# Attention transposes as 64x64 products with the identity, decoding parts one step later, six squares on GpSimd

## The chip, the cores and the metric

The kernel runs on one core of a Trainium2 chip. PE (TensorE) multiplies into PSUM, eight banks of 512 f32 columns on 128 partitions; ACT (ScalarE), DVE (VectorE) and POOL (GpSimd) work on SBUF, the first two on PSUM too; SP (SyncE) issues the transfers. The metric is the device time of one execution in microseconds, the median over runs. "us" is microseconds, "0.90 us" a duration, and a bare position such as 254.95 is microseconds from the start of the span.

## The reference

q, k and v are float32; the four weight arrays are float64, and the kernel reads them as pairs of 32-bit words, which it decodes. Three stages follow each other:

```python
# q, k, v: 8 batches, 8 heads, 576 positions, 64 features; blocks of 64 positions
scores = q_c @ k_c.T / sqrt(64)                 # per batch, head and block
attn = exp(scores - max); attn /= sum(attn) + 1e-9
x = (attn @ v_c)                                # as 4608 tokens x 512 features
# first dense pair: 512 -> 2048 -> 512
x = (max(x @ w_in1, 0) ** 2) @ w_out1
# second dense pair, with another activation
h = x @ w_in2
out = where(h >= 1, h, where(h <= -1, 0, (h + 1) ** 2 / 4)) @ w_out2
```

## The kernel before

**Tokens and slots.** A tile is 128 tokens (two blocks of 64) with all eight heads; there are 36. A unit is a tile's half of four heads (`UT` = 2 units a tile). The first dense product (`plain_h`) works on blocks of 512 tokens, `NBL` = 9 of them, by 16 slices of 128 hidden features; one (block, slice) takes two slots of six matmuls each. The loop at the end walks over slots: in each it issues first what `pe_slot` has put there (matmuls of the dense layers), then what `at_slot` has put there, in the order in which it was put, then one `decode()` where the slot is in `CALLS`. The engines take their instructions in this order. Nothing reorders it.

**Head.** Tiles 0 to 3 (`T0_` = 4) are worked before slot 0, unit by unit, in `head(i)` for i = 0 to 7 and `head_end()`. In step i PE takes `att_a` of unit i+1 (transposes of q and k), `att_b` of i (scores), `att_c` of i-1 (transposes of the attention weights) and `att_d` of i-2 (weights times v); ACT takes `att_ae` (copies of the transposed q and k into qkT), `att_exp`, `att_ce` (copy of the transposed weights into atT) and `att_xh` (result into the high part xh); DVE takes the maxima, the reciprocal of the sums and `att_xl` (low part xl = result - xh); POOL normalizes (`att_n`; the last unit's on DVE). `PARTS[i]` and `LOADS[i]` follow at the end of step i.

**Decoding.** `w_in1` comes as float64 words in 16 pieces. Each piece is turned into a high and a low part in five steps: `piece_u` (ACT: abs; DVE: two operations), `piece_l` (DVE; from part 3 on it also issues the load of a later piece), `piece_b` (DVE), `piece_h` (ACT: rounding copy), `piece_c` (DVE: difference). Pieces 0 to 3 are decoded in the head by `PARTS`, the others by `decode()`.

**Overlapped stage.** From slot 0 on tiles 4 to 35 are worked between the plain matmuls, a tile every `PER` = 8 slots. With g = 6 + 8(t - 5) for tile t: `tile_a` at g-8, `tile_ae` at g-5, `tile_b` at g, `tile_exp` at g and g+1, `tile_n` at g+4, `tile_c` and `tile_ce` at g+6, `tile_d` and `tile_x` at g+8. In slot g PE therefore takes `tile_d` of t-1, `tile_b` of t and `tile_a` of t+1 in a row, in slot g+6 `tile_c` of t alone. Tile 4 has times of its own: scores in slot 1, `tile_c` in slot 10, `tile_d` in slot 12, where tile 5's `tile_c` follows. From slot 28 on the other weights are decoded too, and stored as sums in DRAM.

**PSUM.** Two banks take tag `t`: two buffers of one bank, which psA (transposed q or k) and psC (transposed weights) share. Two banks take `qk` (psB, the scores; in the head the last unit's psD also), two take `d` (psD, the result), two the plain products ph.

**Squares.** `plain_h` ends with relu on ACT and a square, on ACT while the slot is below `U0` = 28 (14 slices), then on POOL; SP stores the result.

Behind slot 288 the rest of the dense layers follows; the change does not touch it.

Of the kernel before, what the change touches and what calls it, by code (L numbers as in the profile page):

```python
# [34 lines left out]
def chunk_attention_moe_moe2(ctx, tc, q, k, v, w_in1, w_out1, w_in2, w_out2, out):  # L35
# [246 lines left out]
    def of_tile(name, u, shape, bufs=1):  # L282

        if (name, u // UT) not in ttile:
            ttile[name, u // UT] = ep.tile(shape, F32, tag=name, name=name, bufs=bufs)
        return ttile[name, u // UT]

    def qkT_of(u):
        t = u // UT
        if t % 2 and t < T0_ and ("qkT", t) not in ttile:  # L290
            ttile["qkT", t] = mp.tile([P, UT, 2, NP, P], F32, tag="q4", name="qkT", padded_shape=[P, 2, 2, 2, P])
        return of_tile("qkT", u, [P, UT, 2, NP, P])
# [39 lines left out]
    def load_v(t):  # L332
        for r, n, b, s in runs_of(t):
            nc.sync.dma_start(out=vt[t % NV][r:r + n], in_=v[b, :, s:s + n, :].rearrange("h s d -> s h d"))

    def att_a(u):

        qkn, h0 = qks[u // UT], u % UT * HU
        pt = pa.tile([P, 2, NP, P], F32, tag="t", name="psA", bufs=2)
        for i in range(2):  # L340
            for p in range(NP):
                nc.tensor.transpose(
                    pt[:, i, p, :], qkn[i][:, h0 + 2 * p:h0 + 2 * p + 2, :].rearrange("p h d -> p (h d)"), ident
                )
        att[u] = pt

    def att_ae(u):
        qkT = qkT_of(u)[:, u % UT]
        pt = att.pop(u)
        nc.scalar.activation(out=qkT[:, 0], in_=pt[:, 0], func=AF.Copy, scale=SCALE)  # L350
        nc.scalar.copy(qkT[:, 1], pt[:, 1])

    def tile_a(t, halves=(0, 1)):

        for i in halves:
            att[t, "a", i] = pt = pa.tile([P, UT, NP, P], F32, tag="t", name="psA", bufs=2)
            for h in range(0, H, 2):
                nc.tensor.transpose(  # L358
                    pt[:, h // HU, h // 2 % NP, :], qks[t][i][:, h:h + 2, :].rearrange("p h d -> p (h d)"), ident
                )  # L360

    def tile_ae(t, halves=(0, 1)):
        qkT = qkT_of(t * UT)
        for i in halves:
            pt = att.pop((t, "a", i))
            if i == 0:
                nc.scalar.activation(out=qkT[:, :, 0], in_=pt, func=AF.Copy, scale=SCALE)
            else:
                nc.scalar.copy(qkT[:, :, 1], pt)

    def att_b(u):

        pt = pa.tile([P, 2, 512], F32, tag="qk", name="psB")
        scores(pt[:, :, 0:2 * CH], qkT_of(u)[:, u % UT])
        att[u] = maxima(pt, 2)

    def scores(pt, qkT):
        for p in range(NP):
            for e in range(2):
                for c in range(2):  # L380
                    nc.tensor.matmul(  # L381
                        pt[rows(p), e, c * CH:(c + 1) * CH],
                        qkT[rows(e), 0, p, rows(c)],
                        qkT[rows(e), 1, p, rows(c)],
                        start=True,
                        stop=True,
                    )
# [30 lines left out]
    def tile_b(t):  # L418
        pt = pa.tile([P, 2, 512], F32, tag="qk", name="psB")
        for i in range(UT):  # L420
            scores(pt[:, :, i * 2 * CH:(i + 1) * 2 * CH], qkT_of(t * UT)[:, i])
        att[t, "b"] = maxima(pt, UT * 2)

    def tile_exp(t, e):
# [6 lines left out]
    def att_n(u):  # L431
        normalize(*att[u], nc.gpsimd if u < T0_ * UT - 1 else nc.vector)

    def turned(pt, s, n):
        for e in range(2):
            nc.tensor.transpose(  # L436
                pt[:, e].rearrange("k p t -> k (p t)"), s[:, e, 2 * n:2 * n + 2].rearrange("q c k -> q (c k)"), ident
            )

    def att_c(u):  # L440
        pt = pa.tile([P, 2, NP, CH], F32, tag="t", name="psC", padded_shape=[P, HU, 2, CH], bufs=2)
        turned(pt, s_of(u), u % UT)
        att[u] = pt

    def att_ce(u):
        nc.scalar.copy(at_of(u)[:, u % UT], att.pop(u))

    def tile_c(t):
        att[t, "c"] = pt = pa.tile([P, UT, 2, NP, CH], F32, tag="t", name="psC", bufs=2)
        for i in range(UT):  # L450
            turned(pt[:, i], s_of(t * UT), i)

    def tile_ce(t):
        nc.scalar.copy(at_of(t * UT), att.pop((t, "c")))

    def att_d(u):

        pt = pa.tile([P, 2, 512], F32, tag="qk" if u == T0_ * UT - 1 else "d", name="psD")
        weigh(pt, u)
        att[u] = pt  # L460
# [13 lines left out]

    def att_xh(u):
        att[u] = x_ops(att[u], u)
        att[u][0]()

    def att_xl(u):
        att.pop(u)[1]()  # L480
# [8 lines left out]
        )  # L489

    def tile_d(t):
        att[t, "d"] = pt = pa.tile([P, 2, 512], F32, tag="d", name="psD")
        for i in range(UT):
            weigh(pt, t * UT + i, i * NP * CH)

    def tile_x(t):
        pt = att.pop((t, "d"))
        ops = [x_ops(pt, t * UT + i, i * NP * CH) for i in range(UT)]
        for n in range(2):
            for o in ops:  # L500
                o[n]()
# [19 lines left out]
    def plain_h(j, fi, part):  # L521
        n = blocks[j][1]
        if part == 0:
            hs[j, fi] = pa.tile([P, n], F32, tag=f"h{(j * NF + fi) % 2}", name="ph")
        ph = hs[j, fi]
        xh, xl = xs[j, part]
        for i in range(2):
            kt = 2 * part + i
            for a, (wi, x) in enumerate(((0, xh), (1, xh), (0, xl))):
                nc.tensor.matmul(  # L530
                    ph,
                    win[fi][wi][:, kt * P:(kt + 1) * P],
                    x[:, i, :],
                    start=(kt == 0 and a == 0),
                    stop=(kt == KT - 1 and a == 2),
                )
        if part == 0:
            return
        del hs[j, fi]
        g = rt(RG[n_r[0] % len(RG)], [P, n], "g")  # L540
        n_r[0] += 1
        nc.scalar.activation(out=g, in_=ph, func=AF.Relu)  # L542
        if cur[0] < U0:
            nc.scalar.square(g, g)
        else:
            nc.gpsimd.tensor_tensor(out=g, in0=g, in1=g, op=ALU.mult)  # L546
        kh, kk = divmod(fi, HF)
        b0 = blocks[j][0]
# [244 lines left out]
    with tc.manual_schedule():  # L793
# [27 lines left out]
        def tiles_until(j):  # L821
# [269 lines left out]
```

## Time and profile before

| | us |
|---|---|
| median of 3 runs (lowest to highest) | 1563.29 (1563.06 to 1563.56) |
| profiled execution | 1563.68 |
| span of the profiled execution | 1561.9 |
| PE busy, share of the span | 1543.7, 99% |
| DVE busy | 1082.7, 69% |
| ACT busy | 871.0, 56% |
| POOL busy | 315.2, 20% |

The span runs from the first to the last instruction; the profiled execution has 1.8 us around it. A PE row's duration includes the emptying of the array, so rows overlap; what a matmul costs in a row of them is the distance between two starts. Names are those of the program's tiles; L579 is a line of the kernel.

### The profile page before, as it was taken

What the parts mean: (1) busy time and instruction counts of PE and PEld (TensorE: products, weight loads), DVE (VectorE), ACT (ScalarE), POOL (GpSimd) and SP (SyncE); (2) the same over time, 40 slices, a digit from 0 to 9 for tenths busy, and PEclk for the clock granted to TensorE, in tenths of its full rate; (3) what the DMA queues carried; (4) which work ended last, traced back from release to release, by engine and by line L of the source; (5) the groups of instructions that cost most, each with busy time, mean ns of one, the idle gap of its engine ahead of it and who ended that gap; (6) DMA issues with size and microseconds to landing.
All of it is one profiled execution on the core that took longest, in us unless ns stands there. A gap on an engine that the chain in (4) does not pass through costs nothing.

```text
span 1561.9 us, 26712 instructions
## 1 busy us (share of the span) xinstructions
PE 1543.7 (99%) x9504; PEld 1360.0 (87%) x9504; DVE 1082.7 (69%) x1405; ACT 871.0 (56%) x1768; POOL 315.2 (20%) x351
## 2 busy tenths in 40 slices
PE   7999999999999999999999999999999999999998
PEld 5788888888888889999999889999999889999998
DVE  5866766676452576777677657767675787878876
ACT  6876666666552444444444566767676534444442
POOL 1036666664334100000000122322210000000000
PEclk9999999999999999999999999999999999999999
DMA  9889999999998972716376775665679982744633
GB/s 209 239 244 301 303 301 308 303 311 299 264 286 242 357 213 85 224 49 199 106 225 198 235 269 175 213 231 192 214 263 296 326 230 69 177 120 117 179 70 48
DMA packets 440677, 339.43 MB, mean 217 GB/s; under 512 B 209632, under 2 KB 410336, under 8 KB 440544
## 3 DMA queue, kind: packets, MB, share of 16 engines
q1 hardware_dynamic: 436832, 337.27, 71.3%
q8 instruction: 75, 1.23, 0.3%
q10 hardware_dynamic: 3712, 0.46, 0.2%
q14 instruction: 58, 0.48, 0.1%
HBM read 195.04 MB, written 142.61 MB: 216 GB/s over the span
## 4 chain that ended last, share of the span: by engine, by line
PE 95%; ACT 2%; DVE 1%; DMA 1%; issue 0%; SPq 0%; POOL 0%; POOLq 0%; ACTq 0%
PE X L579 38%; PE ph L530 24%; PE V L579 19%; PE W L579 9%; PE psA L358 2%; PE psD L467 1%; PE psB L381 1%; PE psC L436 1%; DMA ws<-in_moe_w_in_dram 1%; ACT s L399 1%; DMA w<-w 0%; ACT ih L129 0%; ACT ih L179 0%; ACT g L542 0%; DVE wy L133 0%
## 5 line engine op out<-in xcount | busy, mean ns | idle before, releaser
L579 PE MATMUL X<-oh,w 128*128 128x448 f32 (+1 forms) x1920 | 548.5, 367 | 0.0
L566 ACT CAST oh<-gr 128x896 fp32r<-128x896 f32 (+1 forms) x280 | 270.0, 965 | 319.4 <-PE X L579 142.0
L569 DVE TENSOR_TENSOR ol<-gr,oh 128x896 fp32r<-128x896 f32 (+1 forms) x280 | 312.7, 1118 | 176.3 <-ACT oh L566 163.4
L579 PEld LDWEIGHTS X<-oh,w 128*128 128x128 f32 x1920 | 359.8, 187 | 36.4
L579 PE MATMUL X<-ol,w 128*128 128x448 f32 (+1 forms) x960 | 353.6, 368 | 0.4 <-DVE ol L569 0.4
L579 PE MATMUL V<-oh,w 128*128 128x448 f32 (+1 forms) x960 | 274.2, 367 | 0.0
L530 PE MATMUL ph<-xh,ih 128*128 128x512 f32 x576 | 232.1, 403 | 0.0
L530 PE MATMUL ph<-xl,ih 128*128 128x512 f32 x576 | 225.8, 392 | 0.0
L530 PE MATMUL ph<-xh,il 128*128 128x512 f32 x576 | 225.5, 391 | 0.0
L546 POOL TENSOR_TENSOR g<-g 128x512 f32<-128x512 f32 x130 | 164.6, 1267 | 230.5 <-ACT g L542 205.3
L579 PEld LDWEIGHTS V<-oh,w 128*128 128x128 f32 x960 | 179.9, 187 | 18.2
L579 PEld LDWEIGHTS X<-ol,w 128*128 128x128 f32 x960 | 180.2, 188 | 15.8 <-DVE ol L569 0.8
L573 DVE TENSOR_TENSOR gr<-gr,gr 128x896 f32<-128x896 f32 (+1 forms) x160 | 177.7, 1110 | 1.6 <-DMA gr<-g 1.6
L579 PE MATMUL V<-ol,w 128*128 128x448 f32 (+1 forms) x480 | 176.7, 368 | 0.0
L213 POOL TENSOR_TENSOR lc<-lc 128x128 f32<-128x128 f32 x64 | 37.3, 594 | 495.9 <-DVE t L659 364.6
L579 PE MATMUL W<-oh,w 128*128 128x448 f32 (+1 forms) x480 | 137.1, 367 | 0.0
L542 ACT ACTIVATE g<-ph 128x512 f32<-128x512 f32 x144 | 86.1, 598 | 85.4 <-PE ph L530 57.3
L530 PEld LDWEIGHTS ph<-xl,ih 128*128 128x128 f32 x576 | 108.7, 189 | 23.7
L530 PEld LDWEIGHTS ph<-xh,ih 128*128 128x128 f32 x576 | 108.9, 189 | 21.2 <-ACT g L542 0.2
L530 PEld LDWEIGHTS ph<-xh,il 128*128 128x128 f32 x576 | 109.2, 190 | 20.7
L653 ACT ACTIVATE t<-c,half 128x448 f32<-128x448 f32 (+1 forms) x120 | 81.0, 680 | 49.9 <-DVE c L639 48.7
L399 ACT ACTIVATE s<-psB,m 128x64 f32<-128x64 f32 x288 | 86.4, 318 | 25.3 <-DVE m L393 25.2
(75 smaller groups left out, 1748.1 us busy)
## 6 DMA issues: line engine op xcount, KB each, us to landing
gr<-g SPq DMA_DIRECT2D x128, 448.0 KB, 4.8
w<-w SPq DMA_DIRECT2D x168, 256.0 KB, 5.2
g<-t SPq DMA_DIRECT2D x128, 224.0 KB, 3.0
wu<-in_moe_w_out_dram SPq DMA_DIRECT2D x64, 256.0 KB, 4.9
gr<-g SPq DMA_DIRECT2D x32, 512.0 KB, 6.7
w<-wh SPq DMA_DIRECT2D x32, 448.0 KB, 4.5
w<-wl SPq DMA_DIRECT2D x32, 448.0 KB, 5.1
ws<-in_moe_w_in_dram SPq DMA_DIRECT2D x16, 512.0 KB, 5.3
```

Source lines behind the costliest of these rows:

```text
L213: nc.gpsimd.tensor_tensor(out=c[:, o], in0=c[:, x], in1=c[:, z], op=op)
L358: nc.tensor.transpose(pt[:, h // HU, h // 2 % NP, :], qks[t][i][:, h:h + 2, :].rearrange("p h d -> p (h d)"), ident)
L381: nc.tensor.matmul(pt[rows(p), e, c * CH:(c + 1) * CH], qkT[rows(e), 0, p, rows(c)], qkT[rows(e), 1, p, rows(c)], start=True, stop=True,)
L399: nc.scalar.activation(out=s[:, e, c], in_=sc[:, e, c], func=AF.Exp, bias=m[:, e, c:c + 1], accum_out=z[:, e, c:c + 1],)
L530: nc.tensor.matmul(ph, win[fi][wi][:, kt * P:(kt + 1) * P], x[:, i, :], start=(kt == 0 and a == 0), stop=(kt == KT - 1 and a == 2),)
L542: nc.scalar.activation(out=g, in_=ph, func=AF.Relu)
L546: nc.gpsimd.tensor_tensor(out=g, in0=g, in1=g, op=ALU.mult)
L566: nc.scalar.copy(t[0], raw)
L569: nc.vector.tensor_tensor(out=t[1], in0=raw, in1=f(t[0]), op=ALU.subtract)
L573: eng.tensor_tensor(out=o, in0=x, in1=z, op=ALU.subtract)
L579: nc.tensor.matmul(o, wt_[:, wi, c, :], x[:, i, :], start=first and a == 0, stop=last and a == 2, skip_group_check=True,)
L653: nc.scalar.activation(out=t, in_=h, func=AF.Square, bias=half, scale=0.5)
```

## The change

All transposes of the attention, which PE did with its transpose of a 128x128 block, become products: each 64x64 quarter of the data is the stationary operand, and 64 columns of the identity are moved through, in the quarter of the array that belongs to the data's partitions (r) and to the result's (e). The result of row half r goes to bank r. psA becomes one tile of two banks that all tiles use (q in columns 0 to 255, k in 256 to 511); psC is gone, its products go to columns 256 to 511 of the one psD, whose columns 0 to 255 take the result. The layout of qkT changes to match, and the scores' loop has its column block outermost. The `PARTS` list begins with an empty step, so that each part comes one head step later, and `piece_b` of piece 3 goes into `head_end`. Squares below slot `SQ0` = 12 (six slices) go to POOL.

```diff
     def qkT_of(u):
...
-            ttile["qkT", t] = mp.tile([P, UT, 2, NP, P], F32, tag="q4", name="qkT", padded_shape=[P, 2, 2, 2, P])
+            ttile["qkT", t] = mp.tile([P, 2, UT, NP, P], F32, tag="q4", name="qkT", padded_shape=[P, 2, 2, 2, P])
+    def turn(pt, src, o):
+        for r in range(2):
+            for e in range(2):
+                nc.tensor.matmul(
+                    pt[rows(e), r, o:o + CH], src(r, e), ident[rows(r), rows(r)], start=True, stop=True
+                )
     def att_a(u):
         qkn, h0 = qks[u // UT], u % UT * HU
-        pt = pa.tile([P, 2, NP, P], F32, tag="t", name="psA", bufs=2)
         for i in range(2):
             for p in range(NP):
-                nc.tensor.transpose(
-                    pt[:, i, p, :], qkn[i][:, h0 + 2 * p:h0 + 2 * p + 2, :].rearrange("p h d -> p (h d)"), ident
-                )
+                turn(psA, lambda r, e: qkn[i][rows(r), h0 + 2 * p + e, :], u % UT * 256 + (i * NP + p) * CH)
     def att_ae(u):
...
+        qkT = qkT_of(u)
+        for i in range(2):
+            o = u % UT * 256 + i * NP * CH
+            src = psA[:, :, o:o + NP * CH].rearrange("d r (p t) -> d r p t", p=NP)
+            copy_qk(i, qkT[:, i, u % UT].rearrange("d p (r t) -> d r p t", r=2), src)
     def tile_a(t, halves=(0, 1)):
         for i in halves:
-            att[t, "a", i] = pt = pa.tile([P, UT, NP, P], F32, tag="t", name="psA", bufs=2)
             for h in range(0, H, 2):
-                nc.tensor.transpose(
-                    pt[:, h // HU, h // 2 % NP, :], qks[t][i][:, h:h + 2, :].rearrange("p h d -> p (h d)"), ident
-                )
+                turn(psA, lambda r, e: qks[t][i][rows(r), h + e, :], i * 256 + h // 2 * CH)
     def scores(pt, qkT):
-        for p in range(NP):
-            for e in range(2):
-                for c in range(2):
+        for c in range(2):
+            for p in range(NP):
+                for e in range(2):
                     nc.tensor.matmul(
...
-    def turned(pt, s, n):
+    def turned(u):
+        s, n = s_of(u), u % UT
         for e in range(2):
-            nc.tensor.transpose(
-                pt[:, e].rearrange("k p t -> k (p t)"), s[:, e, 2 * n:2 * n + 2].rearrange("q c k -> q (c k)"), ident
-            )
+            turn(psD, lambda r, c: s[rows(r), e, 2 * n + c, :], 256 + (2 * n + e) * CH)
+    def copied(at, o, n):
+        nc.scalar.copy(
+            at.rearrange("k e p t -> k p e t"), psD[:, :, o:o + n * CH].rearrange("k p (e t) -> k p e t", t=CH)
+        )
     def tile_c(t):
-        att[t, "c"] = pt = pa.tile([P, UT, 2, NP, CH], F32, tag="t", name="psC", bufs=2)
         for i in range(UT):
-            turned(pt[:, i], s_of(t * UT), i)
+            turned(t * UT + i)
     def att_d(u):
-        pt = pa.tile([P, 2, 512], F32, tag="qk" if u == T0_ * UT - 1 else "d", name="psD")
-        weigh(pt, u)
-        att[u] = pt
+        weigh(psD, u, u % UT * NP * CH)
     def tile_d(t):
-        att[t, "d"] = pt = pa.tile([P, 2, 512], F32, tag="d", name="psD")
         for i in range(UT):
-            weigh(pt, t * UT + i, i * NP * CH)
+            att_d(t * UT + i)
...
-        if cur[0] < U0:
+        if SQ0 <= cur[0] < U0:
             nc.scalar.square(g, g)
         else:
             nc.gpsimd.tensor_tensor(out=g, in0=g, in1=g, op=ALU.mult)
...
-    U0, UPER = 28, 5
+    U0, UPER, SQ0 = 28, 5, 12
...
+        psA = pa.tile([P, 2, 512], F32, tag="t", name="psA")
+        psD = pa.tile([P, 2, 512], F32, tag="d", name="psD")
...
         PARTS = (
+            (),
             ((piece_u, 0), (piece_l, 0)),
...
             ((piece_l, 3), (piece_c, 2)),
-            ((piece_b, 3),),
         )
...
             att_xl(u - 2)
+            piece_b(3)
             att_c(u)
             att_d(u - 1)
```

## Rows read from the trace of the kernel before

**Rows 1.** The page's first part: busy us (share of the span) and instructions.
```profile
PE 1543.7 (99%) x9504; PEld 1360.0 (87%) x9504; DVE 1082.7 (69%) x1405; ACT 871.0 (56%) x1768; POOL 315.2 (20%) x351
```

**Rows 2.** Busy time by stretch: from:to, length, engines, granted clock, DMA share, GB/s.
```profile
20.00:30.00 10.00, 8.81 (x114) 5.91 (x113) 8.13 (x21) 9.09 (x44) 1.84 (x3) 1.00 0.96 215
50.00:60.00 10.00, 7.78 (x37) 6.28 (x36) 8.49 (x17) 9.23 (x29) 0.00 (x0) 0.93 0.98 248
200.00:300.00 100.00, 100.00 (x930) 82.64 (x933) 67.79 (x102) 66.40 (x202) 65.74 (x78) 1.00 0.98 302
```

**Rows 3.** PE's waits in 0 to 100 us: total us, times, longest.
```profile
PE psC L436 <- ACT qkT L367: 2.2, 1, 2.2
```

**Rows 4.** PE timeline, one period: start, us, line, operation, tiles, shapes, count.
```profile
254.95 0.39 PE L530 MATMUL ph<-xl,ih 128*128 128x512 f32 x1
255.18 0.60 PE L436 MATMUL psC<-ident,s 128*128 128x128 f32 x4
...
255.85 0.40 PE L530 MATMUL ph<-xh,il 128*128 128x512 f32 x1
...
258.16 0.39 PE L530 MATMUL ph<-xl,ih 128*128 128x512 f32 x1
258.48 0.69 PE L467 MATMUL psD<-atT,vt 64*64 64x64 f32 x32
258.99 0.75 PE L381 MATMUL psB<-qkT 64*64 64x64 f32 x32
259.67 1.09 PE L358 MATMUL psA<-ident,qkn 128*128 128x128 f32 x8
...
260.84 0.40 PE L530 MATMUL ph<-xh,il 128*128 128x512 f32 x1
...
268.78 0.60 PE L436 MATMUL psC<-ident,s 128*128 128x128 f32 x4
```

**Rows 5.** PE timeline around the last psD.
```profile
475.24 0.39 PE L530 MATMUL ph<-xl,ih 128*128 128x512 f32 x1
475.56 0.69 PE L467 MATMUL psD<-atT,vt 64*64 64x64 f32 x32
476.18 0.50 PE L530 MATMUL ph<-xh,ih 128*128 128x512 f32 x1
476.52 0.39 PE L530 MATMUL ph<-xh,il 128*128 128x512 f32 x1
```

**Rows 6.** PE timeline cut at 258.62: the first two rounds of psD.
```profile
258.48 0.34 PE L467 MATMUL psD<-atT,vt 64*64 64x64 f32 x8
```

**Rows 7.** PE timeline at slot 10.
```profile
55.71 0.39 PE L530 MATMUL ph<-xl,ih 128*128 128x512 f32 x1
58.31 0.91 PE L436 MATMUL psC<-ident,s 128*128 128x128 f32 x4 [2.22 <-ACT qkT L367]
...
62.01 0.40 PE L530 MATMUL ph<-xh,il 128*128 128x512 f32 x1
```

**Rows 8.** Groups by line and shape: busy us, mean ns, idle before and its releasers.
```profile
L546 POOL TENSOR_TENSOR g<-g 128x512 f32<-128x512 f32 x130 | 164.6, 1267 | 230.5 <-ACT g L542 205.3 <-DMA g<-g 9.0 <-DMA w<-w 6.7
...
L544 ACT ACTIVATE g<-g 128x512 f32<-128x512 f32 x14 | 8.9, 633 | 0.4
```

**Rows 9.** Timeline of all engines at slot 12.
```profile
63.89 0.66 PE L436 MATMUL psC<-ident,s 128*128 128x128 f32 x4
...
64.74 0.76 DVE L488 TENSOR_TENSOR xl<-psD,xh 128x256 fp32r<-128x256 f32 x2 [2.58 <-ACT xh L487]
```

**Rows 10.** Timeline of all engines in the first unit.
```profile
3.79 0.29 PEld L342 LDWEIGHTS psA<-ident,qkn 128*128 128x128 f32 x2 [0.28 <-DMA qkn<-in_k_dram]
...
4.52 0.38 ACT L350 ACTIVATE qkT<-psA 128x256 f32<-128x256 f32 x1 [2.51 <-PE psA L342]
```

**Rows 11.** PE timeline at the end of the head.
```profile
33.93 0.66 PE L436 MATMUL psC<-ident,s 128*128 128x128 f32 x2
...
35.72 0.80 PE L530 MATMUL ph<-xh,ih 128*128 128x512 f32 x1
```

More of the change, by code (lines that the diff above doesn't have):

```diff
@@ L290, in qkT_of @@
         if t % 2 and t < T0_ and ("qkT", t) not in ttile:
-            ttile["qkT", t] = mp.tile([P, UT, 2, NP, P], F32, tag="q4", name="qkT", padded_shape=[P, 2, 2, 2, P])
-        return of_tile("qkT", u, [P, UT, 2, NP, P])
+            ttile["qkT", t] = mp.tile([P, 2, UT, NP, P], F32, tag="q4", name="qkT", padded_shape=[P, 2, 2, 2, P])
+        return of_tile("qkT", u, [P, 2, UT, NP, P])
     def s_of(u):
@@ L334, in load_v, with copy_qk @@
             nc.sync.dma_start(out=vt[t % NV][r:r + n], in_=v[b, :, s:s + n, :].rearrange("h s d -> s h d"))
+    def turn(pt, src, o):
[4 more added lines that the diff above has]
+                )
     def att_a(u):
         qkn, h0 = qks[u // UT], u % UT * HU
-        pt = pa.tile([P, 2, NP, P], F32, tag="t", name="psA", bufs=2)
         for i in range(2):
             for p in range(NP):
-                nc.tensor.transpose(
-                    pt[:, i, p, :], qkn[i][:, h0 + 2 * p:h0 + 2 * p + 2, :].rearrange("p h d -> p (h d)"), ident
-                )
-        att[u] = pt
+                turn(psA, lambda r, e: qkn[i][rows(r), h0 + 2 * p + e, :], u % UT * 256 + (i * NP + p) * CH)
     def att_ae(u):
[L348 to L351, printed above, removed]
+        qkT = qkT_of(u)
[3 more added lines that the diff above has]
+            copy_qk(i, qkT[:, i, u % UT].rearrange("d p (r t) -> d r p t", r=2), src)
+    def copy_qk(i, out, src):
+        if i == 0:
+            nc.scalar.activation(out=out, in_=src, func=AF.Copy, scale=SCALE)
+        else:
+            nc.scalar.copy(out, src)
     def tile_a(t, halves=(0, 1)):
         for i in halves:
-            att[t, "a", i] = pt = pa.tile([P, UT, NP, P], F32, tag="t", name="psA", bufs=2)
             for h in range(0, H, 2):
-                nc.tensor.transpose(
-                    pt[:, h // HU, h // 2 % NP, :], qks[t][i][:, h:h + 2, :].rearrange("p h d -> p (h d)"), ident
-                )
+                turn(psA, lambda r, e: qks[t][i][rows(r), h + e, :], i * 256 + h // 2 * CH)
     def tile_ae(t, halves=(0, 1)):
@@ L364, in tile_ae @@
         for i in halves:
[L365 to L369, printed above, removed]
+            src = psA[:, :, i * 256:(i + 1) * 256].rearrange("d r (p t) -> d r p t", t=CH)
+            copy_qk(i, qkT[:, i].rearrange("d u p (r t) -> d r (u p) t", r=2), src)
     def att_b(u):
         pt = pa.tile([P, 2, 512], F32, tag="qk", name="psB")
-        scores(pt[:, :, 0:2 * CH], qkT_of(u)[:, u % UT])
+        scores(pt[:, :, 0:2 * CH], qkT_of(u)[:, :, u % UT])
         att[u] = maxima(pt, 2)
     def scores(pt, qkT):
-        for p in range(NP):
-            for e in range(2):
-                for c in range(2):
+        for c in range(2):
+            for p in range(NP):
+                for e in range(2):
                     nc.tensor.matmul(
@@ L420, in tile_b @@
         for i in range(UT):
-            scores(pt[:, :, i * 2 * CH:(i + 1) * 2 * CH], qkT_of(t * UT)[:, i])
+            scores(pt[:, :, i * 2 * CH:(i + 1) * 2 * CH], qkT_of(t * UT)[:, :, i])
         att[t, "b"] = maxima(pt, UT * 2)
@@ L432, in att_n @@
         normalize(*att[u], nc.gpsimd if u < T0_ * UT - 1 else nc.vector)
-    def turned(pt, s, n):
+    def turned(u):
+        s, n = s_of(u), u % UT
         for e in range(2):
-            nc.tensor.transpose(
-                pt[:, e].rearrange("k p t -> k (p t)"), s[:, e, 2 * n:2 * n + 2].rearrange("q c k -> q (c k)"), ident
-            )
+            turn(psD, lambda r, c: s[rows(r), e, 2 * n + c, :], 256 + (2 * n + e) * CH)
[3 more added lines that the diff above has]
+        )
     def att_c(u):
-        pt = pa.tile([P, 2, NP, CH], F32, tag="t", name="psC", padded_shape=[P, HU, 2, CH], bufs=2)
-        turned(pt, s_of(u), u % UT)
-        att[u] = pt
+        turned(u)
     def att_ce(u):
-        nc.scalar.copy(at_of(u)[:, u % UT], att.pop(u))
+        copied(at_of(u)[:, u % UT], 256 + u % UT * 2 * CH, 2)
     def tile_c(t):
-        att[t, "c"] = pt = pa.tile([P, UT, 2, NP, CH], F32, tag="t", name="psC", bufs=2)
         for i in range(UT):
-            turned(pt[:, i], s_of(t * UT), i)
+            turned(t * UT + i)
     def tile_ce(t):
-        nc.scalar.copy(at_of(t * UT), att.pop((t, "c")))
+        copied(at_of(t * UT).rearrange("k u e p t -> k (u e) p t"), 256, UT * 2)
     def att_d(u):
-        pt = pa.tile([P, 2, 512], F32, tag="qk" if u == T0_ * UT - 1 else "d", name="psD")
-        weigh(pt, u)
-        att[u] = pt
+        weigh(psD, u, u % UT * NP * CH)
     def weigh(pt, u, o=0):
@@ L475, in att_xh @@
     def att_xh(u):
-        att[u] = x_ops(att[u], u)
+        att[u] = x_ops(psD, u, u % UT * NP * CH)
         att[u][0]()
@@ L491, in tile_d @@
     def tile_d(t):
-        att[t, "d"] = pt = pa.tile([P, 2, 512], F32, tag="d", name="psD")
         for i in range(UT):
-            weigh(pt, t * UT + i, i * NP * CH)
+            att_d(t * UT + i)
     def tile_x(t):
-        pt = att.pop((t, "d"))
-        ops = [x_ops(pt, t * UT + i, i * NP * CH) for i in range(UT)]
+        ops = [x_ops(psD, t * UT + i, i * NP * CH) for i in range(UT)]
         for n in range(2):
```

## The prediction

> **What bounds the kernel now.** I read the page's first part, then busy time by stretch, then PE's waits, then the PE timeline of one period of the overlapped stage. PE is busy for 99% of the span [rows 1]. By stretch [rows 2] there are three regimes. In the head (to 35.7 us), at 20 to 30 us, PE is 88% busy, but ACT is at 91%, DVE at 81% and the DMA engines at 96%: everything is nearly full. At 50 to 60 us PE has its one real hole, 7.78 of 10 us, while ACT has 9.23. From 80 us on PE is full; at 200 to 300 us it is busy for all of 100 us, with DVE at 68, ACT at 66, POOL at 66 and the DMA engines at 98%. So there an edit is worth what it takes off PE, unless the transfers cannot follow. PE's waits [rows 3] confirm it: they all lie in the first 80 us, and the longest one outside the head is 2.2 us, at psC, for ACT's qkT copy.
>
> **The change part by part.**
>
> *Transposes in the overlapped stage.* A period is 13.60 us: 48 plain matmuls at 0.23 us from start to start, plus two attention blocks [rows 4]. The cost of a block is the distance from the last plain start before it to the second one behind it, less two plain steps (0.46). psC's four transposes: 255.85 - 254.95 - 0.46 = 0.44 us. psD, psB and psA together: 260.84 - 258.16 - 0.46 = 2.22 us.
>
> Behind the change both are blocks of 64x64 products. What such a block costs among plain matmuls is seen where the last psD stands alone: 476.52 - 475.24 - 0.46 = 0.82 us for 32 products, that is eight rounds of the four quarters [rows 5]. A round more costs 0.058 us: 32 starts cover 0.69 us [rows 4], the first 8 of them 0.34 [rows 6], so six rounds cost 0.35. Entering and leaving 64x64 mode is the rest: 0.82 - 8 x 0.058 = 0.36 us.
>
> The new product (64x64 weights from the data, 64 columns of the identity, row quarter outside, column quarter inside, one bank per row half) has the shape, order and type of psD's, so I take psD's price. No row shows a product with the identity in a quarter; its bounds are 0.058 us a round and 0.12, if a round costs as much as one 128x128 transpose does now (psA: 260.84 - 0.23 - 259.67 = 0.94 for eight [rows 4]).
> - psC's 16 products are four rounds: 0.82 - 4 x 0.058 = 0.59, **0.15 more** than now, since a stretch that had no change of mode now has two.
> - psD, psB and psA are 24 rounds in one mode: 0.82 + 16 x 0.058 = 1.75, **0.47 less**. This takes psB's eight rounds at psD's pace. With its old order it needs 0.68 us to the next block's start where psD needs 0.62 [rows 4, 5]; if the new order does not help, 0.06 comes back per tile, 1.8 in all.
>
> The trace shows the switch: psC starts 0.23 behind a plain matmul, psD 0.32 [rows 4], and the last psD needs 0.62 us to the next plain start, of which eight rounds are 0.47 [rows 5]. The Trainium skill, page "TensorEngine Tiling (Array Packing)", Key Properties, says that changing the tiling mode drains the TensorE; this speaks against the psC part, and the trace agrees. Without a drain a tile would gain 1.0 us and not 0.32.
>
> From slot 14 on the large block occurs 29 times and psC 30 times: 29 x 0.47 = 13.6 less, 30 x 0.15 = 4.5 more, **-9.1 us**. Ahead of it the pair psB, psA at slot 6 gains 0.47, a half psA and tile 4's psC lose 0.15 each, and the other blocks gain some 0.3 (psB's order, and at slot 12 psD and psC in one mode): **-0.5**.
>
> *The wait at slot 10.* psC and psA share two buffers; the psC of tile 4 waits until ACT has copied tile 6's psA. It starts at 58.31 instead of 55.94, and the granted clock is then at half (1.2 GHz): plain matmuls come every 0.43 us until 62.01 [rows 7]. The idle time is 2.4 us; psC and seven plain steps take 3.70 us where 0.44 + 7 x 0.23 = 2.05 would do, 1.65 lost. Now psC writes psD, not psA's buffer, so this wait has no cause left. ACT moreover loses six squares, each 0.63 us [rows 8], to a POOL that is idle there [rows 2]. POOL's square takes 1.27 us [rows 8], so a store is issued 0.6 us later, and so is what stands behind it on SP's queue; I cost this at 0, since five buffers of g lie between it and PE and loads are issued a tile ahead (without that cover: 6 x 0.6 = 3.6). What is late next is DVE's normalize of later tiles, with DVE at 85% at 50 to 60 us [rows 2]; the short wait at psC of tile 6 I leave where it is. **-4.0 us** (none of it to all of it).
>
> *One tile psD for psC and psD, one psA for both halves.* In the first unit, ACT's copy of q waits for the transposes of k, which go to other columns of the same bank: k's weights load at 3.79, the copy starts at 4.52 and waited for psA [rows 10]. So I take it that work on one bank is ordered whatever its columns. The Trainium skill, page "PSUM — Partial Sum Buffer", section "PSUM bank collisions raise a hardware error", has the rule: guard by bank and quadrant, not by address. In the steady stage this costs nothing: psC of a tile is issued six slots (8 us) behind the previous psD, whose readers are long done. But at slot 12 psD of tile 4 and psC of tile 5 stand back to back. psC now starts at 63.89; behind the change it has to wait for both xl of tile 4, which end at 64.74 + 0.76 = 65.50 [rows 9]. Queued behind it on PE are all plain matmuls. **+1.6 us**; by column the price is 0, and if the clock falls as at slot 10, 3.3.
>
> *Head.* PE works at the low clock there (two of psC's transposes cover 0.66 us, later four cover 0.60 [rows 4, 11]). Per unit its transposes shrink, but ACT, DVE and the transfers are as full as PE [rows 2], and the order of loads is kept. Moving the decoding parts one step later takes the first wait for weights out of ACT's and DVE's queues and removes no work; on SP the load of part 6, which piece_l of part 3 issues, now stands behind tile 5's q and k (0: its decoding is slots away). piece_b of part 3 fills a hole of DVE behind the last normalize. I estimate that the last unit's weights are normalized 2.1 us earlier (units of 2.7 to 2.8 us in place of 3.0, ACT and DVE being at 8 to 9 of 10 us). Against it, from the last psC to the first plain matmul it takes 1.79 us now [rows 11], with the last psD in the scores' buffer. Now that psD has to wait for the psD before it to be read: copies of 0.3, 0.3 and a subtraction of 0.4 with their handovers, and the last psC waits for one subtraction: +1.4. Net **-0.7** (ends: -3.1 where only the gains come, +1.4 where only the waits do). New access patterns of the copies have as many elements: 0.
>
> **Sum** against the profiled execution: -9.1 - 0.5 - 4.0 + 1.6 - 0.7 = -12.7; 1563.7 - 12.7 = 1551.0 (span 1561.9, 1.8 around it). The median of the runs is 0.4 below the profiled one, so 1550.6.
>
> **The rivals.**
> - *A, the wait moves.* DVE or ACT is late in slots 0 to 20, and PE waits as long as before, at another tile: 1550.6 + 4.0 = 1554.6. For it: DVE at 8.49 and ACT at 9.23 of 10 us; against it: ACT loses 3 us of squares by slot 10 and the buffer is no longer shared.
> - *B, transfers bound the overlapped stage.* At 98% of the DMA engines' time a period 0.3 us shorter asks for what they have left. If 13.6 us is their floor, the gain from slot 28 on (27 of 30 tiles, 8.2 us) is lost: 1559. For it: the share. Against: PE never waits there, and 302 GB/s [rows 2] is a mean.
> - *C, slower: a round of identity products is not four at once.* Price 12 rounds a tile on 31 tiles, 372 in all. At 0.12 us a round 372 x 0.06 = 22 come back: 1573. It decides from 0.034 more a round, that is from 0.092 us. For it: no row shows the form, and psB shows that the order of quarters matters. Against: psD, the same in all but its operand, keeps 0.058 in every block.
> - *D, shorter head, no bank wait*: -2.4 and -1.6 more: 1546.6. The page "TensorE: Matmul & The Clock Gate" of the Trainium skill (Part 4) says that transposes do not count as busy for the clock; no row here can tell, as head steps mix both. If the head came out at the high clock, its first six plain steps would give back 6 x 0.2 = 1.2 us, inside D.
>
> **Numbers.** Forecast 0.62 (own range 1547.5 to 1554.5), A 0.14, B 0.09, C 0.06, D 0.09. What a measurement can tell from no change is 0.2%, 3.1 us. The range is 1546 to 1559: it takes in A, most of D and half of B. Slower by over 0.2% is C alone, 0.06; same is the upper half of B and part of C's lower prices, 0.05; faster 0.89.
>
> **What would show it.** Right: psC's block at 0.59 and the large block at 1.75 us between plain matmuls; a period near 13.3; no idle PE and no half clock at slot 10; about 1.6 us of idle ahead of tile 5's psC, released by DVE's xl; first plain matmul near 35.0. Wrong: rounds over 0.08 us (C), PE waiting for qkn, vt or buffers behind stores (B), idle PE at psC released by POOL or DVE's normalize (A), a psC that follows psD at once (D).

## The result, and the profile after

The changed kernel takes **1586.26 us** (median of 4 runs, 1583.8 to 1591.12) against 1563.32 (4 runs, 1563.06 to 1563.56): ratio 1.0146 [1.0133, 1.0158]. I had forecast 1550.6, within 1546 to 1559. The prediction is wrong in sign. The profiled execution took 1586.09 us (before 1563.68), with a span of 1584.3.

The first part of the page answers to [rows 1].

```profile
PE 1556.6 (98%) x12528; PEld 1367.0 (86%) x12528; DVE 1088.1 (69%) x1405; ACT 867.3 (55%) x1762; POOL 318.4 (20%) x357
```

PE has 3024 instructions more. The groups of the attention's products on PE say where they are (busy us, mean ns, idle before).

```profile
L340 PE MATMUL psA<-ident,qkn 64*64 64x64 f32 x2304 | 47.6, 232 | 8.6 <-DMA qkn<-in_q_dram 4.0 <-issue 2.7 <-ACT qkT L362 1.1
L340 PE MATMUL psD<-ident,s 64*64 64x64 f32 x1152 | 28.1, 236 | 8.5 <-DVE xl L492 4.4 <-DVE s L415 2.2 <-POOL s L415 1.9
L471 PE MATMUL psD<-atT,vt 64*64 64x64 f32 x1152 | 27.4, 233 | 1.2 <-DVE xl L492 1.2
L386 PE MATMUL psB<-qkT 64*64 64x64 f32 x1152 | 26.4, 228 | 3.1 <-issue 1.6 <-ACT s L404 1.6
```

There are 36 tiles, and the code issues 16 products a tile for psB, 16 for psD, 16 for the turned weights and 32 for q and k. The trace has 32, 32, 32 and 64: **each f32 product is two matmul instructions**. The whole transposes of before were one each: four psC and eight psA a tile in [rows 4]. That is 3456 instructions now for 432 then, and 3024 is the difference.

One period of the overlapped stage on PE, answering to [rows 4]:

```profile
253.18 0.39 PE L532 MATMUL ph<-xl,ih 128*128 128x512 f32 x1
253.50 0.69 PE L340 MATMUL psD<-ident,s 64*64 64x64 f32 x32
...
254.46 0.39 PE L532 MATMUL ph<-xh,il 128*128 128x512 f32 x1
...
256.75 0.39 PE L532 MATMUL ph<-xl,ih 128*128 128x512 f32 x1
257.07 0.69 PE L471 MATMUL psD<-atT,vt 64*64 64x64 f32 x32
257.59 0.65 PE L386 MATMUL psB<-qkT 64*64 64x64 f32 x32
258.05 1.11 PE L340 MATMUL psA<-ident,qkn 64*64 64x64 f32 x64
259.10 0.50 PE L532 MATMUL ph<-xh,ih 128*128 128x512 f32 x1
259.44 0.39 PE L532 MATMUL ph<-xh,il 128*128 128x512 f32 x1
...
267.49 0.69 PE L340 MATMUL psD<-ident,s 64*64 64x64 f32 x32
```

Counted as in the prediction, the weights' block costs 254.46 - 253.18 - 0.46 = 0.82 us (0.44 before, 0.59 forecast), the large block 259.44 - 256.75 - 0.46 = 2.23 (2.22 before, 1.75 forecast). The period is 267.49 - 253.50 = 13.99 in place of 13.60.

PE's two longest waits in 36 to 100 us, answering to [rows 3] (engine, tile, line, releaser: us in total, times, longest). The wait of 2.2 us for ACT's qkT is gone, and a longer one stands in its place.

```profile
PE psD L340 <- DVE xl L492: 4.0, 1, 4.0
PE psD L471 <- DVE xl L492: 1.2, 1, 1.2
```

It lies at slot 12, answering to [rows 9]. PE's rows show the turn of tile 5's weights 4.04 us late, and the plain matmuls behind it at steps of 0.43 us:

```profile
67.89 1.14 PE L340 MATMUL psD<-ident,s 64*64 64x64 f32 x32 [4.04 <-DVE xl L492]
...
69.97 0.63 PE L532 MATMUL ph<-xl,ih 128*128 128x512 f32 x1
70.40 0.63 PE L532 MATMUL ph<-xh,ih 128*128 128x512 f32 x1
...
72.90 0.39 PE L532 MATMUL ph<-xh,ih 128*128 128x512 f32 x1
73.13 0.39 PE L532 MATMUL ph<-xh,il 128*128 128x512 f32 x1
```

The windows give the granted clock of that stretch (length, busy us of PE, PEld, DVE, ACT, POOL, clock, DMA share, GB/s): half, that is 1.2 GHz, from 66.0 to 72.8, in and behind PE's pause of 63.85 to 67.89, and full from there on.

```profile
50.00:60.00 10.00, 10.00 (x158) 8.02 (x159) 9.79 (x15) 7.04 (x26) 3.02 (x3) 1.00 0.84 208
66.00:72.80 6.80, 4.91 (x41) 4.02 (x42) 4.72 (x9) 2.49 (x5) 0.00 (x0) 0.50 0.85 276
```

At 50 to 60 us DVE is busy for 9.79 of 10 (8.49 in [rows 2]). DVE's timeline shows why its xl of tile 4, which PE waits for, starts at 67.09 only: the normalize of tile 5 and decoding stand ahead of it, and two operations take twice as long as their like.

```profile
60.87 1.41 DVE L122 SCALAR_TENSOR_TENSOR wy<-ws,wy 128x512 uint32<-128x512 uint32 x1
...
62.64 0.69 DVE L415 TENSOR_TENSOR s<-s,z 128x512 f32<-128x512 f32 x1
63.25 1.53 DVE L183 TENSOR_TENSOR il<-wy,ih 128x512 fp32r<-128x512 f32 x1
...
66.48 0.69 DVE L122 SCALAR_TENSOR_TENSOR wy<-ws,wy 128x512 uint32<-128x512 uint32 x1
67.09 0.75 DVE L492 TENSOR_TENSOR xl<-psD,xh 128x256 fp32r<-128x256 f32 x2
67.75 0.68 DVE L183 TENSOR_TENSOR il<-wy,ih 128x512 fp32r<-128x512 f32 x1
```

In the kernel before, the same normalize came 4.2 us earlier:

```profile
58.47 0.69 DVE L410 TENSOR_TENSOR s<-s,z 128x512 f32<-128x512 f32 x1
```

The two long operations lie on top of one of the squares that moved to POOL:

```profile
60.65 1.08 POOL L548 TENSOR_TENSOR g<-g 128x512 f32<-128x512 f32 x1 [2.63 <-ACT g L544]
62.63 1.59 POOL L548 TENSOR_TENSOR g<-g 128x512 f32<-128x512 f32 x1 [0.90 <-ACT g L544]
```

The best ledger is the start of the same plain matmul in both traces (each trace has 6768 of them; a slot is six, a tile eight slots). Us later than before, in each kernel's profiled run, with the kernels of the next section:

```
slot     after    e1     e2     e3     e4     e5     e6     e7     e8     e9    e10    e11
0        +1.93  +1.09  +0.13  +2.34  -0.48  +1.89  +1.16  -0.07  -0.41  -1.50  +2.34  -0.19
10       +3.56  +2.92  +0.20  +4.56  +0.47  +2.61  +1.92  +1.00  +0.11  -1.84  +4.01  -0.04
12       +0.13  -0.89  -3.23  +1.12  -0.87  -1.21  -1.90  -0.70  -0.30  -5.01  +0.58  -3.85
16       +6.49  +5.79  +3.23  +2.36  -1.16  +2.29  -1.84  -0.91  +0.18  +1.45  +4.61  -3.78
48       +8.87  +5.83  +4.13  +5.34  -1.56  +1.86  -1.78  -0.38  +0.16  -0.87  +7.65  -3.72
112     +11.85  +5.93  +6.21  +8.33  -2.36  +1.06  -2.58  -0.38  +0.16  -6.04 +13.17  -4.52
192     +15.59  +6.07  +8.81 +12.06  -3.36  +0.06  -3.58  -0.38  +0.16  -8.77 +16.94  -5.52
224     +17.09  +8.08  +9.85 +13.99  -3.76  -0.34  -3.98  -0.38  +0.16  -4.09 +19.97  -5.92
256     +22.08 +11.59 +10.90 +15.26  -2.88  -0.73  -4.38  -0.09  +0.09  -2.23 +21.31  -6.31
end     +22.43 +11.57 +11.24 +15.25  -2.94  -0.38  -4.04  +0.02  +0.15  -1.75 +21.31  -6.18
```

For the change: 3.6 us by slot 10, -3.4 at slots 10 and 11, +6.4 at slots 12 to 15, 10.6 from slot 16 to slot 224 (26 tiles at 0.373 a tile, the rest single stops), 5.0 at slots 224 to 255.

### The profile page after: what moved, and what is told of

Its sections match the earlier page's. It is cut to its first block, busy times and chain, and to the rows that moved or that the text cites. A ratio compares the mean times of both kernels' runs of the same rounds, so it can differ in the third digit from the quotient of the medians.

```text
span 1584.3 us, 32684 instructions
## 1 busy us (share of the span) xinstructions
PE 1556.6 (98%) x12528; PEld 1367.0 (86%) x12528; DVE 1088.1 (69%) x1405; ACT 867.3 (55%) x1762; POOL 318.4 (20%) x357
## 4 chain that ended last, share of the span: by engine, by line
PE 92%; DMA 3%; DVE 2%; issue 1%; ACT 1%; SPq 1%; ACTq 0%; DVEq 0%
PE X L581 37%; PE ph L532 23%; PE V L581 19%; PE W L581 9%; PE psA L340 2%; PE psD L471 1%; PE psD L340 1%; DMA qkn<-in_k_dram 1%; PE psB L386 1%; DMA g<-g 1%; ACT s L404 0%; DVE wy L122 0%; DMA gr<-g 0%; DMA wu<-in_moe_w_out_dram 0%; DVE wy L133 0%
```

## The experiments

Each kernel was timed over several rounds against the kernel before on the same chip (medians there 1564.06 to 1564.25).

**e1, e2 and e3: undoing one part of the change.** e1 turns the weights whole again, into the free columns of psD.

```diff
     def turned(u):
...
-            turn(psD, lambda r, c: s[rows(r), e, 2 * n + c, :], 256 + (2 * n + e) * CH)
...
+            o = 256 + e * P
+            nc.tensor.transpose(psD[:, n, o:o + P], s[:, e, 2 * n:2 * n + 2].rearrange("q c k -> q (c k)"), ident)
...
```

> The changed kernel with the attention weights turned by PE's transpose of 128x128 again, written to the free columns of psD; all else as changed. Theory S (every f32 product is two matmuls, so the weights' block is eight rounds with two changes of mode, 0.82 us in place of 0.44, and that is the whole loss of the overlapped stage): the block falls back to 0.44 us, the period from 13.99 to about 13.60, 31 x 0.38 = 12 us less: about 1574. Rival B (the transfers set the period): the period stays near 14 and the time above 1582.

Measured: 1577.32 us (1575.09 to 1580.33), ratio 1.0086 [1.0068, 1.0104], 8.9 us less than the change where theory S had 12. From slot 48 to slot 192 the distance to before grows by 0.24 us in 18 tiles, where the change loses 6.72. So the weights' products alone lose the 0.37 us a tile, and q's and k's products with the new score order come out even. Rival B falls: the period goes back to 13.6 us.

e2 turns q and k whole, with two buffers psA as before, and keeps the weights as products.

```diff
...
-                turn(psA, lambda r, e: qkn[i][rows(r), h0 + 2 * p + e, :], u % UT * 256 + (i * NP + p) * CH)
+                nc.tensor.transpose(
+                    pt[:, i, p, :], qkn[i][:, h0 + 2 * p:h0 + 2 * p + 2, :].rearrange("p h d -> p (h d)"), ident
+                )
...
```

> The changed kernel with q and k turned by PE's transpose again (psA in two buffers of one bank), the weights still by products. Theory S: 16 rounds without a change of mode cost as much as eight transposes with one; the large block goes from 2.23 to about 2.14 us (the gain of the scores' order stays), 30 x 0.09 = 2.7 less. Theory F (PE's longer stream of instructions makes it wait for its own code in the head, 1.6 and 1.8 us there): these two stops go as well, 2 to 3 us less. Together about 1581; S alone 1583.5. Rival C of the prediction (a product with the identity is slower than another of its shape): 5 us or more less from the block alone.

Measured: 1575.31 us (1574.74 to 1575.83), ratio 1.0067 [1.0052, 1.0082], a larger gain than either expectation allowed. The slope falls to 0.26 a tile (slot 48 to 192: 4.68 in 18), so q's and k's products cost 0.11 more than their transposes, 3.4 us in 30 tiles, and rival C, which asked for 5 or more from this block, falls. The rest of the gain lies at both ends: 3.4 us less than the change at slot 10, with no stop of PE of the kind that ends on "issue", and 1.1 us lost at slots 224 to 255 in place of 5.0.

e3 moves the turn of tile 5's weights ahead of tile 4's last product in slot 12.

```diff
         at_slot(10, tile_ce, T0_)
+        at_slot(12, tile_c, T0_ + 1)
...
-            at_slot(g + 6, tile_c, t)
+            if t > T0_ + 1:
+                at_slot(g + 6, tile_c, t)
```

> The changed kernel with one thing moved: in slot 12 the weights' products of tile 5 are issued ahead of the result's products of tile 4 and not behind them, so that they don't wait for tile 4's reads of the same banks. Theory W (the wait of 4.0 us at psD for DVE's xl and the half clock behind it are due to the shared tile): both go, 6 us less, about 1580. Rival: DVE is late anyway there, and PE waits as long at the next product that needs it: 0 to 2 us less.

Measured: 1580.71 us (1578.44 to 1584.53), ratio 1.0104 [1.0086, 1.0123]. Slots 12 to 15 cost 1.24 us in place of 6.36, and the wait of 4.0 us is gone. So that wait came from two products on one psD standing back to back, as the prediction had it, at a price it had too low. Whether the shared bank orders them or the shared tile, no run tells apart.

**e4: the new score order alone**, on the kernel before.

```diff
-        for p in range(NP):
-            for e in range(2):
-                for c in range(2):
+        for c in range(2):
+            for p in range(NP):
+                for e in range(2):
```

> The kernel before with nothing but the scores' loop in the new order (column block outermost). By the blocks: psB's eight rounds take 0.47 in place of 0.55 us, the large block 2.14 in place of 2.22, 32 x 0.08 = 2.6 less: about 1560.8. Rival: the order does nothing without the other edits: 1563.3.

Measured: 1561.04 us (1560.11 to 1563.9), ratio 0.9982 [0.9972, 0.9992]. The slope is -0.10 us a tile from slot 16 to slot 224. The 1.16 us ahead of it are not the order's alone: in this profiled run the clock stayed full behind the wait at slot 10, which in the kernel before it did not. This part of the change gains.

**e5 and e6: what is left when both turns are whole again.** e5 is the changed kernel with the edits of e1, e2 and e3 together; e6 takes the moved squares out of it as well.

```diff
-        if SQ0 <= cur[0] < U0:
+        if cur[0] < U0:
```

> The changed kernel with q, k and the weights transposed whole again (128x128, one instruction each, the weights' into the free columns of psD), and tile 5's weights turned ahead of tile 4's last product at slot 12; the scores' new order, the shared psD, squares on GpSimd and the moved parts stay. Theory S (all of the loss is the 64x64 products with the identity, each an f32 product in two passes, and the wait at slot 12; the rest of the change gains): 1564 - 3.0 (scores' order, as measured alone) - 3.4 (no wait at slot 10) = 1557.5, PE's period in the overlapped stage 13.5, no pause of PE at slots 10 or 12 over 1 us. Rival R (squares on GpSimd and later parts lose by themselves, as DVE is slowed): 1562 or more, with PE waiting 2 us or more for DVE in slots 8 to 16.

> The kernel of e5_both_transposed with the squares of slots 0 to 11 back on ScalarE. Theory P (GpSimd and VectorE get in each other's way at SBUF: the squares on GpSimd make VectorE's operations in slots 0 to 12 some 25% longer, and VectorE is what is late there): VectorE's L122 back from 871 to about 691 ns, time 0 to 2 us less than e5_both_transposed. Rival (ScalarE is what is late there, and the moved squares are what frees it): 2 to 4 us more, with PE waiting for ScalarE's qkT copies or xh at slot 10.

Measured: e5 1563.56 us (1561.06 to 1567.15), ratio 1.0 [0.9991, 1.0009]; e6 1561.0 (1558.78 to 1564.12), ratio 0.9983 [0.9974, 0.9992]. Theory S falls for e5: something else in the change loses, as rival R had it. At slot 16 of the ledger they are 4.1 us apart: in slots 12 to 15 e5 loses 3.5 us and e6 nothing, and 0.7 us stood between them at slot 0 already, where the two programs are still the same, so that much is chance. PE's row at slot 12 of e5:

```profile
63.88 0.63 PE L444 MATMUL psD<-ident,s 128*128 128x128 f32 x4 [1.99 <-DVE s L416]
```

DVE's normalize, which it waits for, takes 1.56 us there, beside one of POOL's squares, which starts at 62.15.

```profile
62.17 1.56 DVE L416 TENSOR_TENSOR s<-s,z 128x512 f32<-128x512 f32 x1
```

One line of DVE's decoding in 36 to 75 us, in e5 and then in e6 (groups by line: busy us, mean ns):

```profile
L122 DVE SCALAR_TENSOR_TENSOR wy<-ws,wy 128x512 uint32<-128x512 uint32 x9 | 7.7, 851 | 0.3
```

```profile
L122 DVE SCALAR_TENSOR_TENSOR wy<-ws,wy 128x512 uint32<-128x512 uint32 x10 | 6.9, 691 | 0.3
```

So theory P holds for this kernel, with 2.6 us a little more than the 2 it allowed. The Trainium skill, page "SBUF — State Buffer", section "SBUF: two separate sides", has the rule behind it: a GpSimd operation and a VectorE operation with two SBUF inputs take one pair of ports by an exclusive lock, and the loser waits. The traces agree: L122 and the normalize have two SBUF inputs, and the ones that start behind a square take 1.41 and 1.56 us where the others take 0.69. In the change the normalize of 62.64 starts with a square and keeps its 0.69, and there the square takes 1.59 us in place of some 1.1. An operation of DVE with one input is longer beside a square as well: L130 at 49.64, which takes 1.26 us and elsewhere 0.42.

**e7 and e8: squares alone, parts alone**, each on the kernel before.

```diff
-        if cur[0] < U0:
+        if SQ0 <= cur[0] < U0:
...
```

> The kernel before with the six squares of slots 0 to 11 on GpSimd and nothing else. My prediction costed this at 0 (within 0.5 us). Theory P (VectorE slowed by 25% while GpSimd squares): PE's wait at slot 10 stays or grows, 1564 to 1567. Rival (ScalarE freed): the wait of 2.2 us at psC for ScalarE's qkT copy goes, with the half clock behind it, 1560 to 1562.

Measured: 1563.69 us (1562.64 to 1565.42), ratio 0.9999 [0.9991, 1.0008]. DVE's L122 is at 851 ns here too, but it isn't what PE waits for: the wait at slot 10, for ACT, shrinks from 2.2 to 1.9 us only, and neither theory's time came. The ledger's +1.00 and -0.91 are mostly the clock of this one profiled run: it rose at 40.3 us (38.1 before) and did not fall at slot 10. The squares cost nothing that the medians show while ACT is late, and 2.6 us (e5 less e6) once the buffer of that wait has been separated and DVE is late.

```diff
         PARTS = (
+            (),
...
-            ((piece_b, 3),),
         )
...
+            piece_b(3)
```

> The kernel before with the decoding parts one step later and nothing else. The prediction: only the ends of the head move, 0 to -2.1 us by the first plain matmul (35.7 to 33.6 us). Rival: the work only changes its place in queues that are full, first plain matmul at 35.7 +- 0.5, and what is late moves into slots 0 to 12: 1563 to 1566.

Measured: 1563.18 us (1561.89 to 1564.29), ratio 0.9994 [0.9985, 1.0003]. The first plain matmul comes 0.41 us earlier, and by slot 16 that is gone. The rival holds: the work changes its place in full queues.

**e9: one matmul for a product.** The products with the identity take the upper half of each f32 word, as bf16.

```diff
-                    pt[rows(e), r, o:o + CH], src(r, e), ident[rows(r), rows(r)], start=True, stop=True
+                    pt[rows(e), r, o:o + CH], src(r, e).bitcast(BF16)[:, 1::2], ident16[rows(r), rows(r)],
+                    start=True, stop=True
...
```

> The changed kernel, where the products with the identity take only the upper 16 bits of each value (its bf16 part, and a bf16 identity), so that each is one matmul instruction; the values turned are cut to bf16, nothing else differs. Theory M (an f32 product is two matmuls, so that the weights' block has 8 rounds and not 4, and q's and k's 16 and not 8, at 0.058 us each): blocks of 0.59 and 1.75 us as predicted, period 13.99 - 12 x 0.058 = 13.3, about 20 us less in the overlapped stage: 1586 - 21 = 1565. Rival C (a round of products with the identity is dear whatever its type): period 13.9 or more, 1583 or more.

Measured: 1561.87 us (1558.61 to 1566.35), ratio 0.9985 [0.9976, 0.9994]. The period on PE:

```profile
183.44 0.39 PE L534 MATMUL ph<-xl,ih 128*128 128x512 f32 x1
183.76 0.32 PE L341 MATMUL psD<-ident,s 64*64 64x64 bf16 x16
...
184.35 0.39 PE L534 MATMUL ph<-xh,il 128*128 128x512 f32 x1
...
186.65 0.39 PE L534 MATMUL ph<-xl,ih 128*128 128x512 f32 x1
186.96 0.69 PE L473 MATMUL psD<-atT,vt 64*64 64x64 f32 x32
187.48 0.65 PE L388 MATMUL psB<-qkT 64*64 64x64 f32 x32
187.94 0.45 PE L341 MATMUL psA<-ident,qkn 64*64 64x64 bf16 x32
188.32 0.50 PE L534 MATMUL ph<-xh,ih 128*128 128x512 f32 x1
188.66 0.39 PE L534 MATMUL ph<-xh,il 128*128 128x512 f32 x1
...
196.71 0.32 PE L341 MATMUL psD<-ident,s 64*64 64x64 bf16 x16
```

Half the matmuls, x16 and x32. The weights' block is 184.35 - 183.44 - 0.46 = 0.45 us, the large one 188.66 - 186.65 - 0.46 = 1.55, the period 196.71 - 183.76 = 12.95. Theory M is right in kind and short by 0.35 a tile, because a bf16 matmul is also cheaper than an f32 one. From the start of psA to the next plain start, 16 rounds of f32 matmuls take 259.10 - 258.05 = 1.05 us in the changed kernel, and 8 rounds of bf16 matmuls 188.32 - 187.94 = 0.38. Rival C, a form that is dear whatever its type, falls. A transpose instruction in the four quarters was not tried.

The total came 3 us under the expectation, not the 10 that the shorter period would add. From slot 192 to slot 256 the kernel gives back 6.5 us, in waits that the kernel before doesn't have. PE's and DVE's in 330 to 460 us, longest of their kind:

```profile
PE psD L341 <- DVE s L417: 4.9, 3, 3.6
PE ph L534 <- ACT g L546: 1.7, 2, 1.5
```

```profile
DVE wq L226 <- DMA w<-wl: 7.9, 2, 5.5
```

Most of it is one stop. DVE waits 5.5 us until a store of decoded weights (wl to w) has left its buffer, its normalize is late, PE waits 3.6 us for that from 370.1 on, and the granted clock is 0.50 from 372.7 to 379.4; the tile of slots 192 to 199 takes 20.22 us. This is the sign that the prediction gave for rival B, buffers behind stores, in a kernel that is fast enough for it. B's floor of 13.6 us a period is not there: most tiles take 12.96.

**e10: the changed kernel with the squares back on ACT**, the edit of e6 alone.

> The changed kernel with the squares of slots 0 to 11 back on ScalarE and nothing else. Theory P (the squares on GpSimd lengthen VectorE's operations, so VectorE's xl of tile 4 is late at slot 12): L122 of VectorE back near 691 ns, the wait at slot 12 under 2.5 us in place of 4.0, slot 16 at +2.5 us against before in place of +6.5: 1582. Rival (the wait at slot 12 is the shared banks alone): wait of 4 us as before, 1586 +- 1.

Measured: 1584.01 us (1580.76 to 1586.55), ratio 1.0125 [1.0111, 1.0139]. Between slots 10 and 16 it loses 0.6 us where the change loses 2.9. The row at slot 12:

```profile
66.90 1.13 PE L340 MATMUL psD<-ident,s 64*64 64x64 f32 x32 [2.59 <-DVE xl L492]
```

The wait is 2.59 us, not 4.04: the shared psD makes the wait, and the slower DVE adds about 1.0 to it, since xl starts at 66.09 in place of 67.09 (the other 0.46 is PE, which comes later here). L122 is back at 691 ns, as theory P had it, but its time, 1582, was not reached: slot 16 is at +4.6, not +2.5, since this run was already at +4.0 at slot 10. Of the 2.3 us won at slots 10 to 15 part is lost later to stops that end on "issue", below. The ratios of e10 and of the change have intervals that overlap, so the medians alone don't tell the two apart.

**e11: own banks.** From the kernel before: the score order, and tiles 4 and on turned whole into psD's free columns, with e3's order at slot 12; head, squares and parts as before.

```diff
...
     def tile_c(t):
-        att[t, "c"] = pt = pa.tile([P, UT, 2, NP, CH], F32, tag="t", name="psC", bufs=2)
+        pt = psd()
         for i in range(UT):
-            turned(pt[:, i], s_of(t * UT), i)
+            o = pt[:, i, 256:512].rearrange("k (e p t) -> k e p t", e=2, p=NP)
+            turned(o, s_of(t * UT), i)
...
```

> The kernel before with two parts of the change alone: the scores' new order, and the weights of tiles 4 and on transposed (whole, as before) into the free columns of psD in place of the buffer shared with psA, tile 5's ahead of tile 4's last product at slot 12. The head is the one before, squares stay on ScalarE, parts where they were. Theory: -3.0 (the order, as measured alone) -3.5 (the wait at slot 10 and the half clock behind it): 1557.5. Rival (the head's length or a later wait takes it back, as in e6_squares_on_act): 1560.5 or more.

Measured: **1557.72 us** (1556.47 to 1560.73), ratio 0.9964 [0.995, 0.9977], the fastest kernel here. At slots 10 and 12 PE does not wait:

```profile
55.90 0.60 PE L436 MATMUL psD<-ident,s 128*128 128x128 f32 x4
...
59.34 0.66 PE L436 MATMUL psD<-ident,s 128*128 128x128 f32 x4
59.92 0.69 PE L475 MATMUL psD<-atT,vt 64*64 64x64 f32 x32
```

It wins 3.8 us at slots 10 and 11 and 0.10 a tile, and keeps both to the end.

## Why the prediction was wrong

**The step that failed** is the count of rounds: "psC's 16 products are four rounds" and "psD, psB and psA are 24 rounds". I took 16 products for the weights and 32 for q and k from the code, and the price from trace rows whose counts I divided by four as they stood; but those rows count matmuls, and an f32 product is two. [Rows 4] had it: psD and psB stand there with x32, for 16 products of the code. The price of a round of matmuls, 0.058 us, and of the change of mode, 0.36, were right. With eight rounds and 32 they give 0.36 + 8 x 0.058 = 0.82 and 0.36 + 32 x 0.058 = 2.22; measured 0.82 and 2.23. The overlapped stage would have come out at 30 x 0.38 + 29 x 0.01 = +11.7 in place of -9.1, and the forecast, with its other terms as they stood, at 1571; nearly all of the other 15 us are in the terms below. Rival C had the size, 1573, under another mechanism. Four products do run at once; each goes through in two matmuls, and e9 shows that halving them, with a cheaper type, turns the loss of 0.37 a tile into a gain of 0.65.

**The score order** was right in direction and a little better than the 0.06 us a tile allowed for: 0.10 (e4).

**The wait at slot 10** went as forecast: -3.4 us against -4.0. e11 shows that this takes the separate buffer, and neither the products nor the moved squares. The 1.65 us of half clock in the term are not sure: the clock fell at this wait in the kernel before and in e8, but not in e4 and e7, which wait 2.3 and 1.9 us there.

**Slot 12**: the mechanism was right (the turn waits for both xl of tile 4, which read other columns of the same psD; e3), the term mis-sized: 1.6 us forecast, 6.4 measured. I priced the wait by DVE's xl of before, at its place in DVE's queue then. PE came to the turn at 63.85, as before (63.89), but xl started at 67.09 and not at 64.74. DVE's normalize of tile 5 came at 62.64 in place of 58.47, so the 2.58 us that DVE had free ahead of xl in [rows 9] were gone. By e10 the moved squares make up about 1.0 us of the 2.35 by which xl was later. The clock fell to half for 6.8 us in and behind the pause; even "if the clock falls" I had 3.3.

**Squares on GpSimd at 0** is half right: 0 on the kernel before (e7), 2.6 us where DVE ends last (e5 less e6). The reason given, that POOL is idle there, looked at the wrong engine. **The moved parts** alone are worth nothing: the first plain matmul comes 0.41 us earlier, and that is gone by slot 16 (e8).

**The head**: -0.7 forecast, +1.9 measured at slot 0. The wait on the shared psD came about as priced: the last psD waits 1.23 us for DVE's xl and the last turn 0.33, against +1.4. The turn of a unit's weights did shrink, to 0.48 us from start to start at the half clock (23.97 to 24.45), where the two transposes took 0.61 (24.80 to 25.41). What no term of the prediction had are stops of PE in the middle of a block, which end on "issue", 3.6 us in all:

```profile
20.37 0.34 PE L386 MATMUL psB<-qkT 64*64 64x64 f32 x6 [1.57 <-issue]
...
27.12 0.81 PE L340 MATMUL psA<-ident,qkn 64*64 64x64 f32 x21 [1.80 <-issue]
...
37.01 0.71 PE L471 MATMUL psD<-atT,vt 64*64 64x64 f32 x16 [1.23 <-DVE xl L492]
```

e2 and e9, which have products with the identity in the head but no such stop, reach slot 0 at +0.13 and -1.50. The stops aren't the whole of it: e5, with neither such products nor stops there, comes at +1.89, and e6, the same program up to there, at +1.16. How the head's loss divides stays open.

**Slots 0 to 9** cost 1.6 us, where the prediction had a part of its -0.5. About 1.0 of it is the clock: in the change plain matmuls come at steps of 0.43 us until 42.1 (granted clock 0.50 from 37.7 to 42.0), that is for 4.5 us from the first one at 37.65, and in the kernel before until 38.1, for 2.4 us. Rival D's case, a head that comes out at the high clock, did not come. (The 1.00 of [rows 2] for 20 to 30 us is no measured clock: that trace has no record of it before 38.1, and the steps of 0.43 us up to there show the half clock.)

**Late in the stage**, slots 224 to 255, the change loses 5.0 us that no step foresaw: PE waits 1.83 us for DVE's normalize, and DVE had waited 4.56 until a store (wq to q) had left its buffer. e1 loses 3.5 there, 1.7 of it in a stop that ends on "issue", e3 1.3, e2 1.1, e10 1.3. A delay of a store that comes in some runs would agree with the wide spread of the change's runs, but it stays open.

## What to carry to other kernels

Before pricing a product by a row of the trace, divide the row's count by the number in the code: the same call can be one instruction as a transpose and two as an f32 product. When two uses are put on one tile of PSUM, look for the one place where they stand back to back, and price it by the queue of the engine that frees it. Moving work to an idle engine is free only if the engine that shares its ports is not the late one.

## What the runs showed of the hardware

- A round of four 64x64 f32 products costs about 0.116 us (two rounds of matmuls at 0.058). In bf16, taking off the 0.15 us of leaving the mode (0.62 - 0.47, as in the prediction), it costs (0.38 - 0.15) / 8 = 0.029, a quarter. The Trainium skill, page "FP8 and Floating Point Precision", section "TensorE Precision Notes", says that true FP32 takes four passes through the array; the ratio agrees, though the trace shows two instructions and not four.
- Stops of PE that end on "issue", mostly in the middle of a block of products, add up to 4.3 us in the first 480 us of the change, 8.1 in e10, 3.8 in e3 and 1.7 in e1; none in the kernel before and the others. They go with the instructions that the core loads. That queue's row is in the change (98 packets in e3 and e10 too) and then in e11 (75 packets before and in e4 to e8 too, 83 in e2, 85 in e9, 90 in e1):

```profile
q8 instruction: 98, 1.61, 0.4%
```

```profile
q8 instruction: 75, 1.23, 0.3%
```

That PE waits for its own code there is an inference from this order; no run took the load away by itself.
